# A chunked attention and phase-MLP kernel: the phase weight loaded by SyncE in fp32 and cast on chip, and another order of all work

## The chip, the cores and the metric

The kernel runs on one core of one Trainium2 chip. The time is device microseconds of one execution; the figure given for a kernel is the median of its runs. Lower is better.

## The reference

Two parts follow each other. The first is attention in chunks of 64 rows, the second mixes tokens and channels with cosines and sines.

```python
# q, k, v: (8, 8, 576, 64)
scores = (1 / sqrt(64)) * q_c @ k_c.T            # per batch, head and chunk of 64 rows
attn = softmax(scores)
x = (attn @ v_c), heads side by side             # (8, 576, 512)

theta = x @ w_theta                              # (512, 512)
zr, zi = x * cos(theta), x * sin(theta)
y = w_tok_r @ zr + w_tok_i @ zi                  # (576, 576) over the tokens
u = x + y
out = u + max(u @ w_ch, 0)                       # float32
```

## The kernel before, in words

The eight batches are taken as four pairs, numbered 0 to 3. The 1152 rows of a pair are nine tiles of 128 rows: groups A and B (two tiles each) of the first batch, C and D of the second, and M, one tile made of the last 64 rows of both. Nearly everything is computed in fp16 with sums in fp32.

The program is written out by hand. `ORDER` is a list of steps, and the last loop of the kernel runs through it under a manual schedule; each step records its instructions at once, so the order of the list is the order in each engine's queue. Each engine takes its own queue in order and waits at an instruction until what it needs is there. A step has the form `kind.pair-and-group.bank`; the PSUM banks (eight, of 512 fp32 columns) are chosen in the list too. A digit 0 or 1 at the end of a kind means one half of a step. The kinds that matter here:

- `qF`, `kF`, `q`, `k` and `v` (lines L181, L194, L222 and L232) load by POOL's queue, which casts fp32 to fp16 on the way. A whole group's q or k is 512 KB in HBM and 256 KB on chip. `lw` loads the token weights (L243), `lc` the channel weight (L254), `lt` the phase weight theta (`load_theta`, L251). From pair 1 on, `gate` (L170) makes POOL copy one number of the latest reciprocal of `norm` before a load is issued, which ties the loads to the progress of the attention.
- `F` (L301), `FL` (L316), `L` (L339) and `N` (L335) turn q and k on TensorE by transposes against an identity. `F` does a group with 64 transposes of 64x64, `FL` with 32 of 128x64. For group M, `L` takes 16 and `N` 8.
- `tq` and `tqA` copy the turned q from PSUM (VectorE L368, ScalarE L370), `tkV` and `tkA` the turned k (L368, L372).
- `S` is the scores (L405), `e` the exponential (L422), `V` the product with v (L440), with a column of ones for the sum, and `n` the reciprocal and the scaling (VectorE, L452 and L454).
- `X` (L478) and `Q` (L487) turn x: 8 transposes of 128x128, or 32 of 64x64. `U` and `R` do the same with u. `xA`, `xV`, `uA` and `uV` copy the result on ScalarE or VectorE (L501).
- `H` is x times theta (L518), `g` cosine and sine (ScalarE, L532 and L536), `z` the two products (VectorE, L548 and L549).
- `TW` turns the token weights (L269). For pair 0, `YA` to `YD` and `YM` mix the tokens directly (L604); for pairs 1 to 3 it is done by seven products `Ka` to `Kg` and `Km` over differences of blocks (L693), with the differences made by `ja` to `jd` and the results taken by `ra` to `rh` (VectorE, L712). `Y` is the mixing of group M (L590), `y` the sum with x.
- `W` is u times the channel weight (L518), `w` adds the positive part (VectorE, L733), `s` and `sA` store by SyncE's and ScalarE's queue (L748 and L744).
- `D` issues dummy products of zeros on TensorE (L280); `pe` and `pg` call the exponential's or the sine's table on ScalarE.

The pool `nat` has ten buffers, which groups' q and k, the token weights, the differences of `j` and the last output tiles take in turn.

Of the kernel before, what the change touches and what calls it, by code (L numbers as in the profile page):

```python
# [9 lines left out]
FP32 = mybir.dt.float32  # L10
# [18 lines left out]
n0.1C kF.2A lc.00 tkA.1B YA.0A.6 V1.1A.0 n1.1A V0.1A.4 YB.0A.6 v.1M V1.1C.0 n0.1A S.1B.2 L.1M.4
qF.2C e.1B X.1A.5 qF.2D xA.1A n1.1C X.1C.0 kF.2C YM.0A.6 U.0D.1 H.1A.2 xV.1C pg.00 g.1A tq.1M  # L30
uV.0D H.1C.0 tkV.1M kF.2D F.1D.5.4 tkA.1D y.0A jw.01 v.2A R.0C.6 g.1C tq.1D uV.0C YA.0B.2 S.1D.4
V0.1B.6 YM.0B.2 n0.1B z.1C YB.0B.2 e.1D y.0B FL.2A.0 qF.2B tqA.2A V1.1D.6 q.2M V0.1D.4 n0.1D
W.0D.2 S.1M.4 k.2M n1.1D w.0D X.1D.6 kF.2B TW.04.7 tkA.2A e.1M v.2D twV.04 V1.1M.0 V0.1M.1
S.2A.2 xA.1D e.2A V1.1B.4 n1.1B n0.1M z.1A H.1D.6 n1.1M X.1B.5 pg.00 g.1D xV.1B W.0C.2 w.0C
ja.1C R.0A.0 X.1M.4 uA.0A sA.0C z.1D qF.3A jc.1D U.0B.5 H.1B.6 uA.0B v.2C g.1B xA.1M W.0A.0
Ka.1A.2 w.0A F.2C.4.5 F.2D.0.1 ra.1A tq.2D tkA.2C tkA.2D sA.0D jb.1D qF.3D Y.0M.7 V0.2A.0 n0.2A
z.1B tqA.2C H.1M.6 y.0M N.2M.4 tkA.2M g.1M Kf.1C.2 S.2D.0 tqA.2M F.2B.7.6 V1.2A.4 rc.1C n1.2A
z.1M v.3D e.2D tqA.2B kF.3D Kg.1D.2 rg.1B X.2A.0 xV.2A Ke.1C.4 re.1D tkA.2B v.2M Km.1D.2 qF.3B
U.0M.1 rf.1D H.2A.6 pg.00 g.2A uV.0M Kc.1D.4 jd.1B S.2C.0 pe.00 e.2C q.3M v.2B s.0A rd.1C
V0.2D.6 n0.2D Y.1M.2 S.2B.6 kF.3A y.1M V0.2C.0 n0.2C e.2B k.3M Kb.1B.4 z.2A V1.2C.6 qF.3C kF.3C  # L40
S.2M.0 e.2M n1.2C W.0B.2 rb.1A V1.2D.0 n1.2D Q.2C.6 W.0M.4 U.1C.5 w.0B s.0B v.3A w.0M U.1A.0
uV.1C X.2D.1 xA.2C H.2C.2 xV.2D V1.2M.4 V0.2B.6 uA.1A V0.2M.5 pg.00 g.2C n1.2M n0.2B H.2D.0
W.1A.6 g.2D n0.2M Q.2M.4 xA.2M F.3A.2.3 F.3D.0.1 z.2C w.1A V1.2B.4 n1.2B tkA.3D W.1C.6 tqA.3A
ja.2C z.2D X.2B.1 w.1C H.2M.2 xA.2B Kd.1B.4 tkA.3A tqA.3D g.2M H.2B.6 rh.1B v.3C s.0M S.3A.0
jb.2D kF.3B R.1D.2 Ka.2A.4 g.2B v.3B Ke.2C.6 z.2M uA.1D ra.2A Kf.2C.4 F.3C.2.3 e.3A V0.3A.0
jc.2D tkA.3C re.2D n0.3A tqA.3C rc.2C Kc.2D.6 rd.2C V1.3A.0 n1.3A S.3D.2 e.3D Kg.2D.4 z.2B rg.2B
S.3C.6 s.1A e.3C Q.3A.0 W.1D.2 U.1B.6 v.3M Km.2D.4 xA.3A H.3A.0 w.1D rf.2D V0.3C.2 n0.3C R.1M.4
uV.1M uA.1B W.1B.6 sA.1C jd.2B F.3B.2.3 N.3M.4 pg.00 g.3A z.3A w.1B Kb.2B.0 tqA.3B tkA.3B
V1.3C.2 tqA.3M rb.2A S.3B.6 pe.00 e.3B Y.2M.5 n1.3C tkV.3M Q.3C.0 xA.3C V0.3D.6 y.2M n0.3D
S.3M.2 W.1M.4 e.3M w.1M U.2C.5 uA.2C V1.3D.0 V1.3M.2 n1.3D s.1B V0.3M.3 n0.3M n1.3M H.3C.6 pg.00  # L50
g.3C V0.3B.0 sA.1M Q.3D.4 xV.3D Kd.2B.2 n0.3B rh.2B V1.3B.0 n1.3B R.2D.6 uA.2D W.2C.4 w.2C
# [10 lines left out]
def kernel(  # L62
# [22 lines left out]
    GT = 2 * P  # L85
# [20 lines left out]
    nat = ctx.enter_context(tc.tile_pool(name="nat", bufs=10))  # L106
# [60 lines left out]
    def gate(p):  # L167

        if p and marks:
            nc.gpsimd.tensor_copy(out=seen, in_=marks.pop())  # L170
            marks.clear()

    def load_qk(p, g, which, plain, f=None):
        j0, bb, s0 = GROUPS[g]
        gate(p)
        if (p, g) not in nats:
            nats[p, g] = nat.tile([P, 2, 2 * DM], FP16, name="qk16", tag="nat")
        if plain is None:
# [12 lines left out]
        if bb is None:
            t = t[:, 0:DM].rearrange("p (h d) -> p h d", h=H)
            for b in range(2):
                nc.gpsimd.dma_start(  # L194
                    t[half[b]], ap[2 * p + b, :, s0 : s0 + CH, :].rearrange("h s d -> s h d")
                )
            return
        if plain:
            t = t.rearrange("p (j h d) -> p j h d", j=2, h=H)
            for j in range(2):  # L200
                t0 = s0 + j * P
                nc.gpsimd.dma_start(
                    t[:, j, hs],
                    ap[2 * p + bb, :, t0 : t0 + P, :].rearrange("h s d -> s h d"),
                )
            return

        nc.gpsimd.dma_start(
            t.rearrange("p (h x) -> p h x", h=H)[:, hs],
            ap[2 * p + bb, :, s0 : s0 + GT, :].rearrange(  # L210
                "h (p s) d -> p h (s d)", s=2
            ),
        )
# [525 lines left out]
    def store(p, g, f, queue):  # L739
# [71 lines left out]
    with tc.manual_schedule():  # L811
        for step in ORDER:
# [5 lines left out]
            p, g = int(at[0]), int(at[1]) if at[1].isdigit() else at[1]  # L818
# [36 lines left out]
```

## Time and profile before

| | |
|---|---|
| median of 3 runs | 203.94 us (202.31 to 204.08) |
| the profiled execution | 205.1 us, of which the span of the instructions is 203.3 us |
| TensorE busy | 186.4 us (92%), 3567 matmuls |
| VectorE / ScalarE / POOL busy | 150.3 / 124.4 / 83.3 us |
| loads by POOL's queue | 65408 packets, 16.54 MB, 85.9% of 16 engines' span |
| stores by SyncE's and ScalarE's queues | 4.72 MB each, 6.4% and 6.5% |
| granted TensorE clock | 0.999 |

The span starts with the first instruction of the program and ends with the last; the execution has 1.8 us around it. In the views, L numbers are lines of the kernel before, and a DMA's landing is the time at which its completion was signalled. The busy time of TensorE counts dummies too.

### The profile page before, as it was taken

How to read it: one execution, taken by the hardware profiler on the slowest of the kernel's cores; microseconds unless marked ns; L12 is line 12 of the kernel's file. 1: busy time of each engine (PE TensorE's matmuls, PEld its weight loads, DVE VectorE, ACT ScalarE, POOL GpSimd, SP SyncE). 2: the span in 40 equal slices, each digit the busy share in tenths (PEclk: the TensorE clock that was granted, in tenths of full speed). 3: DMA queues.
4: the chain of work that ended last, by engine and by line, in shares of the span. 5: the costliest groups of instructions: out<-in, count | busy, mean ns of one | idle time of the engine just before them, and what ended most of it. 6: DMA issues, size and time to landing. Idle time of an engine off the chain costs nothing.

```text
span 203.3 us, 7900 instructions
## 1 busy us (share of the span) xinstructions
PE 186.4 (92%) x3567; PEld 99.6 (49%) x3567; DVE 150.3 (74%) x238; ACT 124.4 (61%) x150; POOL 83.3 (41%) x134
## 2 busy tenths in 40 slices
PE   7677587999989979999999999999999999999990
PEld 2345445555455545555455564455555544445530
DVE  0042738975766869989988888979988899889480
ACT  2354577995168869679673978956889366001510
POOL 7875957749959675105956137002000000000000
PEclk9999999999999999999999999999999999999999
DMA  5999999999999999962999929505121002004875
GB/s 62 177 191 146 157 141 196 195 175 121 167 178 182 175 128 104 221 223 23 136 141 129 228 108 124 34 3 77 59 106 41 19 3 103 0 0 157 298 286 194
DMA packets 70433, 26.48 MB, mean 130 GB/s; under 512 B 47232, under 2 KB 65792, under 8 KB 70400
## 3 DMA queue, kind: packets, MB, share of 16 engines
q0 software_dynamic: 65408, 16.54, 85.9%
q10 hardware_dynamic: 2496, 4.72, 6.5%
q1 hardware_dynamic: 2496, 4.72, 6.4%
q8 instruction: 28, 0.46, 0.9%
q14 instruction: 5, 0.04, 0.1%
HBM read 33.06 MB, written 9.44 MB: 209 GB/s over the span
## 4 chain that ended last, share of the span: by engine, by line
PE 84%; DMA 4%; POOL 3%; issue 3%; ACT 2%; DVE 1%; ACTq 0%; POOLq 0%
PE ps L518 32%; PE ps L693 21%; PE ps L604 8%; DMA qk<-in_k_dram 4%; PE ps L590 4%; PE ps L478 4%; PE ps L440 3%; PE ps L301 3%; PE ps L487 3%; PE ps L405 3%; POOL qk L181 2%; PE ps L269 2%; POOL v L232 1%; ACT kT L372 1%; PE ps L316 1%
## 5 line engine op out<-in xcount | busy, mean ns | idle before, releaser
L232 POOL DMA_DIRECT2D v<-in_v_dram x48 | 36.3, 778 | 3.6 <-DMA qk<-in_k_dram 2.0
L518 PE MATMUL ps<-wch,uT 128*128 128x512 f16 x144 | 34.1, 380 | 1.2 <-issue 1.2
L518 PE MATMUL ps<-wtheta,xT 128*128 128x512 f16 x144 | 34.5, 380 | 0.0
L712 DVE TENSOR_TENSOR x<-ps,x 128x1024 f16<-128x1024 f32 x24 | 29.1, 1221 | 4.6 <-PE ps L693 4.1
L501 ACT COPY uT<-ps 128x1024 f16<-128x1024 f16 (+1 forms) x14 | 13.6, 982 | 25.8 <-PE ps L487 18.7
L733 DVE SCALAR_TENSOR_TENSOR o<-ps,x 128x1024 f32<-128x1024 f32 (+1 forms) x20 | 22.2, 1115 | 6.7 <-PE ps L518 6.4
L454 DVE TENSOR_TENSOR x<-ps,recip 128x512 f16<-128x512 f32 (+1 forms) x40 | 25.5, 638 | 1.4
L532 ACT ACTIVATE cos<-ps,pihalf 128x1024 f16<-128x1024 f32 (+1 forms) x22 | 21.1, 959 | 6.8 <-PE ps L518 5.8
L422 ACT ACTIVATE eT<-ps 128x1024 f16<-128x1024 f32 (+1 forms) x18 | 16.5, 926 | 11.5 <-PE ps L405 11.2
L372 ACT COPY kT<-ps 128x1024 f16<-128x1024 f16 (+1 forms) x18 | 16.3, 922 | 9.6 <-PE ps L301 5.5
L518 PEld LDWEIGHTS <-uT 128*128 128x128 f16 x144 | 13.1, 98 | 16.2 <-issue 1.7
L518 PEld LDWEIGHTS <-xT 128*128 128x128 f16 x144 | 12.9, 98 | 13.6
L536 ACT ACTIVATE sin<-ps 128x1024 f16<-128x1024 f32 (+1 forms) x22 | 19.0, 865 | 0.0
L693 PE MATMUL ps<-z,wT 128*128 128x512 f16 x72 | 18.8, 379 | 0.0
L170 POOL COPY seen<-recip 1x1 f32<-1x1 f32 x16 | 3.2, 199 | 37.4 <-DVE recip L452 37.4
L452 DVE RECIPROCAL recip<-ps 128x8 f32<-128x8 f32 (+1 forms) x40 | 7.9, 198 | 12.7 <-PE ps L440 11.9
L604 PE MATMUL ps<-z,wT 128*128 128x512 f16 x72 | 16.9, 380 | 0.1
L368 DVE COPY qT<-ps 128x1024 f16<-128x1024 f16 (+2 forms) x11 | 6.4, 581 | 14.3 <-PE ps L316 9.3
L693 PE MATMUL ps<-zsum,wsum 128*128 128x512 f16 x72 | 16.7, 379 | 0.2 <-DVE x L712 0.2
L693 PEld LDWEIGHTS <-wsum 128*128 128x128 f16 x96 | 9.1, 98 | 10.5 <-issue 0.2
L693 PEld LDWEIGHTS <-wT 128*128 128x128 f16 x96 | 9.1, 98 | 10.3
L370 ACT COPY qT<-ps 128x1024 f16<-128x1024 f16 (+2 forms) x12 | 9.9, 823 | 6.5 <-PE ps L316 5.8
(68 smaller groups left out, 294.3 us busy)
## 6 DMA issues: line engine op xcount, KB each, us to landing
qk<-in_q_dram POOLq DMA_DIRECT2D x16, 256.0 KB, 6.0
qk<-in_k_dram POOLq DMA_DIRECT2D x16, 256.0 KB, 6.7
out_dram<-o ACTq DMA_DIRECT2D x8, 512.0 KB, 4.9
out_dram<-o SPq DMA_DIRECT2D x8, 512.0 KB, 3.7
v<-in_v_dram POOLq DMA_DIRECT2D x40, 64.0 KB, 5.3
v<-in_v_dram POOLq DMA_DIRECT2D x16, 128.0 KB, 5.7
wnat<-in_moe_w_tok_r_dram POOLq DMA_DIRECT2D x2, 288.0 KB, 5.8
wnat<-in_moe_w_tok_i_dram POOLq DMA_DIRECT2D x2, 288.0 KB, 6.3
```

What stands on the lines that cost most here:

```text
L232: nc.gpsimd.dma_start(v16[rows, slot + tile, :, 0:D], v[2 * p + bb, :, t0 : t0 + m, :].rearrange("h s d -> s h d"),)
L372: nc.scalar.copy(out=t.rearrange("p x s c -> p x (s c)").rearrange("p x (c s) -> p x c s", s=n), in_=ps.rearrange("p x s c -> p x c s"),)
L422: nc.scalar.activation(out=eT.rearrange("p h r e c -> p (h r e) c"), in_=ps, func=AF.Exp, scale=scale)
L454: nc.vector.tensor_tensor(out=tokens(p, g, "x")[:, :, f * NE * D : (f + 1) * NE * D].rearrange("p c (h d) -> p c h d", h=NE), in0=psv[:, 0 ...
L501: (nc.vector.tensor_copy if how == "V" else nc.scalar.copy)(out=to.rearrange("p b (r c) -> p b r c", c=CH), in_=psv)
L518: nc.tensor.matmul(ps[:, a * DM : a * DM + cols.stop - cols.start], xT[:, b0 + a, db, :], weight[:, db, cols], start=(db == 0), stop=(db = ...
L532: nc.scalar.activation(out=cos[:, 0:n].rearrange("p a e -> p (a e)"), in_=pin, func=AF.Sin, bias=pihalf, scale=1.0,)
L536: nc.scalar.activation(out=sin[:, 0:n].rearrange("p a e -> p (a e)"), in_=pin, func=AF.Sin)
L604: nc.tensor.matmul(ps[:, a * DM : a * DM + DM], wT[:, kt, t0 : t0 + P], zs[bb], start=(done + k == 0), stop=(done + k == NK - 1),)
L693: nc.tensor.matmul(ps[:, a * DM : a * DM + DM], wt, zt, start=fresh and i == 0, stop=i == len(terms) - 1, skip_group_check=to in ("x", "z"),)
L712: nc.vector.tensor_tensor(out=u, in0=st[p]["ps_k", frm], in1=u, op=ALU.add)
L733: nc.vector.scalar_tensor_tensor(out=o, in0=ps[:, 0 : n * m].rearrange("p (j d) -> p j d", j=n), scalar=0.0, in1=u, op0=ALU.max, op1=ALU.add,)
```

## The change

The phase weight is no longer loaded by POOL with a cast on the way. `load_theta` takes two buffers of `nat`, and SyncE issues two loads of 512 KB in fp32 into them, without a wait ahead of them. A new step `ct` casts a half to fp16: `ctA1` the second half on ScalarE, `ctV0` the first half on VectorE.

`ORDER` is another one throughout. The groups of pair 0 come as C, D, A, B, M (before: A, D, C and B, M). Eight whole groups are turned by `F` and six by `FL` (before 13 and 1); `X` is used 12 times and `Q` twice (before 8 and 6), `U` and `R` 8 times each (before 6 and 10), with group M's counted apart; all of group M's turns of q and k are `N`. Five q copies go from VectorE to ScalarE, four u copies from ScalarE to VectorE. There are 43 dummies (before 33), 30 of them ahead of the first turn, and one table call fewer. TensorE has 3233 pairs of weight load and matmul instead of 3567.

```diff
 ORDER = """
-qF.0A kF.0A id.00 init.00 D.12.0 qF.0D D.5.0 FL1.0A.0 kF.0D FL0.0A.2 tqA1.0A tq0.0A tkA1.0A
-S1.0A.0 tkA0.0A F.0D.7.6 tq.0D tkA.0D D.5.2 S.0D.2 e1.0A S0.0A.4 e0.0A v.0A qF.0C D.2.0 V0.0A.0
-qF.0B V1.0A.4 n0.0A kF.0B D.6.0 FL0.0B.0 e.0D FL1.0B.2 kF.0C F.0C.6.7 tkA0.0B tqA0.0B n1.0A
-X1.0A.4 tkA.0C tq1.0B v.0D X0.0A.5 D.3.0 V0.0D.0 tq.0C q.0M k.0M n0.0D lt.00 xV0.0A tkA1.0B
-S1.0B.2 V1.0D.6 n1.0D e1.0B S.0C.0 L0.0M.2 L1.0M.3 e.0C tkV0.0M tkV1.0M X.0D.5 xV.0D tq1.0M
-tqA0.0M S0.0B.0 e0.0B S0.0M.6 S1.0M.0 e1.0M H.0D.2 xV1.0A e0.0M v.0C V0.0C.0 V1.0C.4 pg.00 g.0D
-n0.0C n1.0C H1.0A.7 H0.0A.6 v.0B V1.0B.0 n1.0B v.0M lw.02 Q.0C.4 xA.0C g1.0A V0.0M.2 n0.0M g0.0A
-V0.0B.0 V1.0M.3 H.0C.4 lw.00 qF.1C kF.1C n0.0B X0.0B.0 n1.0M qF.1A kF.1A X1.0B.1 z.0D xV1.0B
-Q.0M.2 xA.0M qF.1B kF.1B v.1C TW.02.6 twV.02 H.0M.3 g.0C TW.03.1 twA.03 q.1M k.1M xV0.0B z1.0A
...
-Q.3B.0 xV.3B R.2B.6 z.3C uA.2B H.3D.2 g.3D R.2A.0 ja.3C uA.2A Q.3M.6 xA.3M z.3D jb.3D H.3B.4
-Ka.3A.2 ra.3A H.3M.0 g.3M z.3M Ke.3C.6 Kf.3C.2 sA.2C re.3D rc.3C W.2A.0 g.3B z.3B w.2A Kc.3D.6
-rd.3C W.2D.4 w.2D jc.3D Kb.3B.0 W.2B.4 jd.3B Kg.3D.2 rb.3A Kd.3B.0 rg.3B Km.3D.2 w.2B R.3A.6
-rh.3B s.2B Y.3M.4 rf.3D s.2A y.3M uA.3A sA.2D R.3C.0 R.3D.2 R.3B.6 W.3A.4 uA.3C w.3A W.3C.0 w.3C
-uA.3B sA.1D U.3M.4 uA.3D W.3D.2 s.3A w.3D W.3B.0 sA.3C R.2M.2 sA.3D uV.3M w.3B s.3B W.3M.4 w.3M
-s.3M uA.2M W.2M.7 w.2M sA.2M
+qF.0C lt.00 id.00 qF.0D kF.0C init.00 D.12.0 D.18.0 FL.0C.0 kF.0D ctA1.00 tqA.0C FL.0D.2 tkA.0D
+tq.0D tkA.0C D.8.6 S.0D.6 e.0D S.0C.0 qF.0A kF.0A FL1.0A.2 tkA1.0A v.0D D.2.4 V0.0D.4 n0.0D
+V1.0D.6 n1.0D D.3.4 X.0D.4 xV.0D e.0C tqA1.0A FL0.0A.0 tq0.0A tkA0.0A v.0C V0.0C.6 n0.0C ctV0.00
+S0.0A.0 S1.0A.2 e1.0A e0.0A qF.0B kF.0B FL1.0B.4 q.0M tq1.0B FL0.0B.6 tq0.0B k.0M V1.0C.2 n1.0C
+N0.0M.0 N1.0M.1 tkV1.0M tkA1.0B S1.0B.4 tqA0.0M X.0C.2 tkA0.0B tkV0.0M S0.0M.6 e1.0B e0.0M
+tq1.0M v.0A xV.0C V1.0A.0 S1.0M.4 e1.0M v.0M S0.0B.2 e0.0B v.0B V0.0A.6 n0.0A H.0D.4 V0.0M.2
+pg.00 g.0D V1.0M.3 n1.0A X1.0A.0 H.0C.6 g.0C lw.02 lw.00 qF.1C kF.1C V1.0B.4 qF.1B n0.0M V0.0B.1
+xV1.0A X0.0A.0 n1.0M H1.0A.3 qF.1A kF.1A xV0.0A kF.1B H0.0A.0 v.1B X.0M.6 n0.0B g1.0A TW.02.1
+n1.0B X0.0B.7 TW.03.4 xA.0M v.1A X1.0B.3 H.0M.6 z.0D twV.03 TW.00.4 z1.0A xA0.0B H0.0B.7 g0.0A
+v.1C twV.02 xA1.0B z.0C qF.1D kF.1D F.1C.0.1 YD.0D.2 twA.00 g.0M lc.00 tkA.1C YC.0D.2 TW.01.4
+q.1M k.1M H1.0B.1 g0.0B tq.1C v.1D F.1A.0.6 z.0M z0.0A lw.04 g1.0B twV.01 YM.0A.4 z1.0B z0.0B
+tkA.1A v.1M YA.0A.4 v.2B YM.0D.2 YB.0A.4 qF.2C tqA.1A qF.2D kF.2D y.0D S.1A.6 qF.2B y.0A FL.1B.0
+pe.00 e.1A S.1C.2 V0.1A.4 n0.1A YD.0C.6 e.1C YM.0C.6 V0.1C.2 FL.1D.4 n0.1C jw.00 tkA.1B qF.3A
+kF.3A tqA.1B S.1B.0 e.1B V1.1A.2 tqA.1D tkA.1D YC.0C.6 U.0A.0 kF.2C n1.1A uV.0A YA.0B.2 V1.1C.0
...
+W.0D.0 N.2M.2 ra.1A tkA.2M Kf.1C.4 z.1M Ke.1C.6 tqA.2M w.0D rc.1C tqA.2A v.2A S.2A.0 e.2A re.1D
+jc.1D FL.2D.2 tqA.2D tkA.2D jd.1B Kc.1D.6 rd.1C V0.2A.0 n0.2A S.2D.2 e.2D Kg.1D.4 Kb.1B.6 sA.0B
+rg.1B F.2B.0.1 Km.1D.4 v.2D R.1C.2 rb.1A sA.0C tkA.2B V1.2A.6 n1.2A uA.1C tqA.2B rf.1D Y.1M.1
+qF.3D V0.2C.2 n0.2C X.2A.0 y.1M S.2B.6 e.2B V1.2D.4 n1.2D W.1C.2 S.2M.4 w.1C qF.3C kF.3C V1.2C.6
+n1.2C xA.2A H.2A.0 e.2M pg.00 g.2A R.0M.2 V0.2D.4 V0.2M.6 U.1A.7 uV.0M W.0M.3 s.0D n0.2D X.2D.2
+V1.2M.4 xA.2D uV.1A w.0M V1.2B.0 n1.2B U.1D.5 n1.2M X.2C.7 n0.2M s.1C uA.1D xA.2C H.2D.2 Q.2M.0
+g.2D F.3A.4.5 V0.2B.6 k.3M xV.2M H.2C.0 g.2C Kd.1B.2 n0.2B X.2B.6 z.2A z.2D xA.2B Ka.2A.0 tqA.3A
+kF.3D z.2C W.1A.6 tkA.3A H.2M.4 s.0M rh.1B H.2B.2 g.2M ja.2C g.2B ra.2A v.3D jb.2D Kf.2C.0 w.1A
...
+rh.2B xV.3C V1.3B.0 Y.2M.4 n1.3B z.3A z.3D V0.3B.0 n0.3B y.2M R.2C.2 uA.2C H.3C.6 W.2C.2 g.3C
+R.2A.0 uA.2A Q.3B.4 Ka.3A.6 w.2C R.2B.0 xA.3B uA.2B z.3C ja.3C jb.3D s.1M Q.3M.4 xA.3M H.3B.2
+W.2B.0 jc.3D g.3B ra.3A H.3M.5 z.3B Ke.3C.2 g.3M re.3D Kf.3C.6 z.3M rc.3C sA.1B jd.3B s.1D w.2B
+sA.2B W.2A.4 Kc.3D.2 w.2A rd.3C Kg.3D.6 rg.3B Kb.3B.0 Kd.3B.2 rb.3A Km.3D.6 R.3A.0 Y.3M.4 s.2D
+uA.3A rh.3B rf.3D R.3D.0 y.3M uV.3D R.3B.6 R.3C.2 uV.3B W.3A.4 w.3A s.2C uV.3C W.3B.0 U.2M.7
+sA.2A w.3B W.3D.4 w.3D uV.2M s.3A W.3C.0 w.3C s.3B U.3M.2 uA.3M s.3D sA.3C W.2M.7 w.2M sA.2M
+W.3M.2 w.3M s.3M
 """.split()
...
     v16 = glob.tile([P, 2 * NT, H, VP], FP16, name="v16")
+    wraw = []
     wnat = {}
...
     def load_theta():
-        nc.gpsimd.dma_start(wtheta16, moe_w_theta.rearrange("(a p) e -> p a e", p=P))
+        for a in range(2):
+            t = nat.tile([P, 2, DM], FP32, name="wraw", tag="nat")
+            wraw.append(t)
+            nc.sync.dma_start(
+                t, moe_w_theta[a * GT : a * GT + GT, :].rearrange("(a p) e -> p a e", p=P)
+            )
+
+    def cast_theta(a, copy):
+        copy(out=wtheta16[:, 2 * a : 2 * a + 2], in_=wraw[a])
...
+        "ctA": lambda p, g, f: cast_theta(f, nc.scalar.copy),
+        "ctV": lambda p, g, f: cast_theta(f, nc.vector.tensor_copy),
```

More of the change, by code (lines that the diff above doesn't have):

```diff
@@ L23 @@
-n0.0C n1.0C H1.0A.7 H0.0A.6 v.0B V1.0B.0 n1.0B v.0M lw.02 Q.0C.4 xA.0C g1.0A V0.0M.2 n0.0M g0.0A
-V0.0B.0 V1.0M.3 H.0C.4 lw.00 qF.1C kF.1C n0.0B X0.0B.0 n1.0M qF.1A kF.1A X1.0B.1 z.0D xV1.0B
-Q.0M.2 xA.0M qF.1B kF.1B v.1C TW.02.6 twV.02 H.0M.3 g.0C TW.03.1 twA.03 q.1M k.1M xV0.0B z1.0A
-z.0C H1.0B.0 v.1A g.0M z0.0A qF.2A v.1D TW.01.6 twV.01 H0.0B.1 g0.0B z.0M TW.00.4 F.1C.3.2 tq.1C
-twA.00 jw.00 YD.0D.6 g1.0B z1.0B YC.0D.6 F.1A.0.1 tkA.1C S.1C.2 pe.00 e.1C YM.0C.4 tq.1A YM.0D.6
-y.0D YC.0C.4 tkA.1A z0.0B F.1B.0.1 qF.1D kF.1D V0.1C.2 v.1B S.1A.6 lw.04 tq.1B YD.0C.4 e.1A y.0C
@@ L29 @@
[L29 to L51, printed above, removed]
-Q.3B.0 xV.3B R.2B.6 z.3C uA.2B H.3D.2 g.3D R.2A.0 ja.3C uA.2A Q.3M.6 xA.3M z.3D jb.3D H.3B.4
@@ new lines @@
+kF.3A tqA.1B S.1B.0 e.1B V1.1A.2 tqA.1D tkA.1D YC.0C.6 U.0A.0 kF.2C n1.1A uV.0A YA.0B.2 V1.1C.0
+qF.2A y.0C S.1D.4 e.1D kF.2A X.1A.7 YB.0B.2 q.2M V0.1D.4 n1.1C V1.1B.0 xA.1A n0.1D n1.1B YM.0B.2
+y.0B kF.2B H.1A.6 TW.04.0 twV.04 k.2M N.1M.5 tq.1M X.1C.4 U.0B.0 tkV.1M pg.00 g.1A uV.0B W.0A.2
+z.1A V0.1B.0 n0.1B S.1M.6 pe.00 e.1M w.0A Y.0M.5 V1.1D.6 n1.1D v.2M s.0A xA.1C X.1B.0 H.1C.2
+pg.00 g.1C xV.1B v.3C X.1D.0 jw.01 y.0M xV.1D z.1C v.3B W.0B.6 U.0D.5 U.0C.0 H.1D.2 uA.0D
+F.2C.1.4 uV.0C w.0B g.1D tqA.2C V0.1M.0 n0.1M V1.1M.5 n1.1M W.0C.6 X.1M.5 H.1B.2 xA.1M v.2C
@@ new lines @@
+tkA.2C ja.1C z.1D w.0C H.1M.0 g.1B jb.1D Ka.1A.4 z.1B S.2C.6 q.3M g.1M F.2A.3.2 tkA.2A e.2C
+W.0D.0 N.2M.2 ra.1A tkA.2M Kf.1C.4 z.1M Ke.1C.6 tqA.2M w.0D rc.1C tqA.2A v.2A S.2A.0 e.2A re.1D
[3 more added lines that the diff above has]
+n1.2C xA.2A H.2A.0 e.2M pg.00 g.2A R.0M.2 V0.2D.4 V0.2M.6 U.1A.7 uV.0M W.0M.3 s.0D n0.2D X.2D.2
@@ new lines @@
+V1.2M.4 xA.2D uV.1A w.0M V1.2B.0 n1.2B U.1D.5 n1.2M X.2C.7 n0.2M s.1C uA.1D xA.2C H.2D.2 Q.2M.0
+g.2D F.3A.4.5 V0.2B.6 k.3M xV.2M H.2C.0 g.2C Kd.1B.2 n0.2B X.2B.6 z.2A z.2D xA.2B Ka.2A.0 tqA.3A
+kF.3D z.2C W.1A.6 tkA.3A H.2M.4 s.0M rh.1B H.2B.2 g.2M ja.2C g.2B ra.2A v.3D jb.2D Kf.2C.0 w.1A
+qF.3B v.3A S.3A.6 jc.2D rc.2C z.2M e.3A F.3C.4.5 tkA.3C Ke.2C.2 Kg.2D.0 kF.3B re.2D tqA.3C
+FL.3D.6 z.2B tqA.3D rg.2B Kc.2D.2 rd.2C U.1M.5 Km.2D.0 rf.2D tkA.3D S.3D.6 sA.1A U.1B.4 v.3M
+e.3D W.1D.2 uA.1B w.1D uA.1M N.3M.0 tqA.3M V0.3A.6 V1.3A.4 U.2D.1 uA.2D Kb.2B.2 n1.3A n0.3A
@@ new lines @@
+X.3A.1 tkA.3M rb.2A W.1M.0 w.1M S.3M.6 xA.3A V0.3D.4 e.3M n0.3D F.3B.2.3 tqA.3B W.2D.0 jd.2B
+V1.3D.4 w.2D n1.3D S.3C.6 tkA.3B e.3C H.3A.2 V0.3C.0 V0.3M.7 V1.3M.4 n1.3M n0.3C pg.00 g.3A
+W.1B.5 X.3D.4 n0.3M w.1B xV.3D Kd.2B.0 V1.3C.2 S.3B.4 H.3D.6 n1.3C Q.3C.2 pe.00 e.3B pg.00 g.3D
+rh.2B xV.3C V1.3B.0 Y.2M.4 n1.3B z.3A z.3D V0.3B.0 n0.3B y.2M R.2C.2 uA.2C H.3C.6 W.2C.2 g.3C
+R.2A.0 uA.2A Q.3B.4 Ka.3A.6 w.2C R.2B.0 xA.3B uA.2B z.3C ja.3C jb.3D s.1M Q.3M.4 xA.3M H.3B.2
+W.2B.0 jc.3D g.3B ra.3A H.3M.5 z.3B Ke.3C.2 g.3M re.3D Kf.3C.6 z.3M rc.3C sA.1B jd.3B s.1D w.2B
```

## The prediction

> **What bounds the kernel now.** I read the page's engine line first, then busy time in six stretches, then the chain of waits, then the DMA landings and the instruction queue's packets.
>
> ```profile
> PE 186.4 (92%) x3567; PEld 99.6 (49%) x3567; DVE 150.3 (74%) x238; ACT 124.4 (61%) x150; POOL 83.3 (41%) x134
> ```
>
> ```profile
> core 0: us, PE busy (x) PEld busy (x) DVE busy (x) ACT busy (x) POOL busy (x), PEclk, DMA share, GB/s
> 0.00:25.30 25.30, 17.73 (x465) 10.40 (x465) 8.16 (x21) 11.11 (x17) 19.91 (x33) 1.00 1.45 146
> 25.30:41.00 15.70, 14.08 (x281) 8.18 (x276) 11.24 (x28) 12.82 (x19) 10.59 (x18) 1.00 1.49 179
> 41.00:75.00 34.00, 31.91 (x758) 17.82 (x744) 23.81 (x41) 22.86 (x27) 25.96 (x43) 1.00 1.71 162
> 75.00:125.00 50.00, 49.75 (x922) 27.02 (x922) 44.25 (x69) 38.53 (x45) 24.68 (x40) 1.00 1.15 142
> 125.00:198.00 73.00, 72.90 (x1176) 36.16 (x1173) 62.17 (x82) 39.09 (x45) 2.21 (x4) 1.00 0.33 86
> ```
>
> TensorE is the bound from 25.3 us to 198 us: 49.75 of 50.00 and 72.90 of 73.00 us busy. No other engine is near its limit over a whole stretch. What can be won lies ahead of 25.3 us, in the idle 3.7 us of the next two stretches, or in TensorE's own work. The last matmul ends at 197.9; 5.4 us of adding and storing follow.
>
> ```profile
> 8.18 8.83 DMA qk<-in_k_dram
> 17.00 0.39 issue
> 17.40 0.65 PE ps L316 x16
> ...
> 27.38 0.55 issue
> ...
> 33.97 0.43 issue
> ...
> 58.03 0.81 issue
> ...
> 68.38 1.01 PE ps L316 x32
> ...
> 71.39 1.21 issue
> ...
> 92.00 1.24 DVE x L712
> ...
> 95.16 0.45 PE ps L478 x8
> ...
> 118.28 1.08 PE ps L301 x128
> ...
> 160.54 0.64 PE ps L487 x64
> ```
>
> Columns: start, us, what. Two things stop TensorE: the load stream (group B's k at 17.0) and pauses called "issue" with no releaser. The pauses sit at TensorE's records 705, 961, 1217, 2241 and 2753 in order: each 193 more than a multiple of 256. The instruction queue brings 28 packets of 16 KB, 256 instructions each, so a pause is a block of instructions that came late. Ahead of 75 us, while the load queue is full, a block's packet begins about 4 us after the block before it was entered, and the block is usable about 2.5 us after that; five of ten blocks made TensorE wait, 3.9 us together.
>
> **The change, part by part.**
>
> *Theta (L250 to 251).* Before, POOL issues it at 18.57, and it lands at 24.40, 2.85 us behind the transfer ahead of it; everything after it in the queue (v.0C, v.0B, v.0M, lw) is that much later. After, SyncE issues two fp32 halves of 512 KB at once. The nearest row is a 512 KB store by SyncE at 147.98: first packet 0.89 us after issue, 256 packets of 2 KB at 87 ns, so 1.4 us of all 16 engines. Two halves are 2.8 us of engine time from about 1.8 us on. The load queue's first packet starts at 2.75, and it moves 32 and 177 packets in the slices 2 to 3 and 3 to 4 us against 395 in the next one. So about 1.55 us of the 2.8 fall into free time, and 1.25 us delay the loads. Bounds: 0.5 (all but the overlap is free) to 2.85 (nothing is). I take 1.2, as the idle slices are counted. The stream past pair 0 is then 2.85 - 1.2 = 1.65 us earlier.
>
> The Trainium skill speaks against the move: "DMA: Bandwidth & Descriptors", section "Issuing engines are not separate DMA queues", says that all issuers share the same 16 engines and that spreading saves only issue time. By that alone the delay is the full 2.85 us and the start gains nothing. No run here shows it either way; the idle slices above are what it leaves out.
>
> *Casts.* Half 1 is a ScalarE copy (1.01 us by the 128x1024 copies), first in ScalarE's queue and ahead of tqA.0C. Theta is through by about 6 us, tqA.0C can start at 10.9, so nothing waits. Half 0 is a VectorE copy after n0.0C, about 20.8. No row has its shape: 0.69 (fp16 copy) to 1.22 us (fp32 input), I take 1.0. Behind it stands tq1.0B, for S1.0B; both hide under the wait for v.0A at 24.9. Without that cover it costs its 1.0 us.
>
> *The start in the new order.* 30 dummies (12 at 0.37, 18 at 0.24 us) end at 10.0. q and k of C and D land by 10.01 + 1.2 = 11.2. H.0D now stands behind V1.0A and V0.0A. Ahead of v.0A stand just the 2816 KB that end with k.0M before, at 21.55; with 2.1 us for v itself and 1.2 delay it lands at 24.9, and H.0D starts at 25.4 (25.3 before), with V.0C and X.0C already done. From there the old order lost 0.55 and 0.43 (issue) and 0.65 us (V0.0B for an x of VectorE); the new one has its data in time up to F.1C. k.1C lands at 38.89 - 1.65 = 37.2; YD.0D can start at 37.9, with TW.01 (0.72) and H1.0B (0.87) left over: as good as 39.5, against 41.14. I book -1.4, keeping 0.2 for small waits. By the bounds of the delay: -2.1 to +0.25.
>
> *TensorE's work after 41 us.* A whole "four long" turning (FL) takes 1.01 for 32 transposes, the old F 1.08 to 1.20 for two of 64, so 0.41 more each. After the start there are FL.1B, 1D, 2D, 3D against FL.2A: +1.24. Five Q or R (0.32 each) become X or U (0.45): +0.65. One L (0.57) becomes N (0.45): -0.12. Sum +1.8 (1.5 to 2.1). The 10 added dummies lie in the wait for loads.
>
> *Instruction blocks.* 3567 matmul and weight pairs become 3233. What decides is where the blocks begin. With TensorE's work from the rows above, the new order has 5.6, 6.3, 8.3, 4.0, 8.0, 6.3 and 10.1 us of work between its block borders from V1.0B to U.0C, against some 6.3 us for a block while the loads run. One stands out: the border in YD.0C, 4.0 us after the one in YM.0D. It waits 1.0 to 3.1 us, by blocks that came in 5.0 to 7.1; I take 2.0, and 0.2 for the one at 6.3. Before, the pauses past 41 us were 0.81 + 1.21 = 2.0. Net +0.2; bounds -2.0 (the load queue is thinner, no waits) to +2.5.
>
> The Trainium skill has this fetch in "Runtime: NRT & Kernel Launch", section "Instruction fetch mechanics": blocks of 256 instructions, the crossing mostly hidden. The size agrees; hidden it is not, by the pause of 1.21 us. Were it hidden, this term would be -2.0.
>
> *Other engines.* Five q copies go from VectorE (0.69) to ScalarE (1.02), four u copies back; one sine table load goes. Neither engine becomes a bound: per us of TensorE's work, VectorE has less to do up to any point of the new order than of the old. One new close gate: v.2D waits on POOL for n0.2A's reciprocal, which stands behind rd.1C (1.22) on VectorE. From the end of Kc.1D: 1.5 us to that, 0.5 for POOL, 5.1 from first issue to last landing (94.03 to 99.12 before): 7.1, where V1.2D is due after 8.7. I book 0.4 (0 to 2). Behind V1.2D all of TensorE's queue stands. Tail: the last step is W, w and two small stores as before; 0.
>
> Sum: -1.4 + 1.8 + 0.2 + 0.4 = **+1.0**. The profiled execution has a span of 203.3 and 205.1 us in all, 1.2 above the median of 203.94. Span 204.3, and median 204.9.
>
> **The rivals.**
> - *Theta nearly free and blocks in time.* For it: the idle slices, and 334 fewer pairs. Against: the 4.0 us interval. -2.1 + 1.8 - 2.0 + 0 = -2.3: 201.6.
> - *Theta's megabyte delays the loads by all it takes.* Both queues are shares of the same 16 engines (section 3 of the profile's page), so each packet of theta is one that the loads have to wait for. (The rule that the Trainium skill gives in "DMA: Bandwidth & Descriptors", section "Issuing engines are not separate DMA queues", leads here.) For it: the DMA row is at 9 from 5 us on. Against: the first 4 us are idle. +0.25 + 1.8 + 0.2 + 0.4 = +2.7: 206.6. It decides once v.0A lands after 25.5.
> - *The gate of v.2D.* If VectorE comes to n0.2A with three operations of 1.22 still ahead instead of one, V1.2D waits 2.4 - 1.6 margin, and the later groups gated behind v.2D the same: with the 2 us of the upper bound, +1.0 - 0.4 + 2.0 = +2.6: 206.5. For it: VectorE is at 44.25 of 50 us there. Against: it has more slack in the new order.
>
> **How the numbers follow.** Forecast 0.50, own range 203.0 to 206.5; free theta 0.20; full delay 0.15; gate 0.15. A measurement here can tell about 1%, 2.0 us. Faster: 0.14 of the first rival and 0.03 of the forecast, 0.17. Slower: 0.21 of the two slow rivals and 0.10 of the forecast, 0.31. Within 1%: 0.52. The range for 8 in 10 takes in all three rivals' times and the ends of the unknown costs: 201.4 to 207.8.
>
> **What would show it.** Right: theta landed by 7 us, k of C or D by 11.5, H.0D at 25 to 26, YD.0D at 37.5 to 38.5; one pause of 1 to 3 us in YD.0C; TensorE without gaps after 75 us; four L316 groups of 1.0 us. Wrong: v.0A after 26, a pause at V1.2D, gaps of TensorE past 100 us, or no pause at all.

## The result, and the profile after

| | before | changed |
|---|---|---|
| median of 20 runs each | 203.94 us | 205.49 us |
| lowest and highest run | 201.76 and 208.15 us | 204.39 and 207.04 us |
| ratio, 95% interval | | 1.0106 (1.0080 to 1.0132) |
| profiled execution, and its span | 205.1, 203.3 us | 205.49, 203.7 us |

The changed kernel is slower, by 1.6 to 2.7 us by the ratio. The ratio compares runs within 1.5% of a kernel's lowest, which leaves out six of the 20 of before and none of the changed kernel's; by plain medians the difference is 1.55 us, 0.8%. The profiled execution of before, at 205.1 us, was 1.2 us above its median and that of the changed kernel is at its median, so the two spans, 0.4 us apart, show less than the change costs.

Line numbers are 9 higher than before (those of the loads of q, k and v 1 higher; in e2 and e11 all are 1 higher). The engine line of the page:

```profile
PE 192.6 (95%) x3233; PEld 105.2 (52%) x3233; DVE 148.9 (73%) x236; ACT 124.7 (61%) x151; POOL 81.6 (40%) x130
```

TensorE is busier by 6.2 us with 334 fewer pairs. Part of that is dummies, and part is turns that ran at a granted clock of one half, from 21.8 to 25.3 us. The stretches say where:

```profile
core 0: us, PE busy (x) PEld busy (x) DVE busy (x) ACT busy (x) POOL busy (x), PEclk, DMA share, GB/s
0.00:25.30 25.30, 20.85 (x364) 12.41 (x365) 7.31 (x19) 11.34 (x16) 19.06 (x32) 0.93 1.60 173
25.30:41.00 15.70, 15.32 (x279) 9.03 (x276) 12.56 (x30) 14.55 (x23) 11.60 (x19) 1.00 1.37 176
41.00:75.00 34.00, 34.00 (x593) 19.26 (x592) 24.12 (x44) 23.29 (x29) 24.33 (x38) 1.00 1.64 156
75.00:125.00 50.00, 49.16 (x906) 27.39 (x905) 42.28 (x65) 36.70 (x41) 25.66 (x42) 1.00 1.19 143
125.00:198.00 73.00, 73.00 (x1101) 37.11 (x1098) 61.82 (x82) 38.86 (x45) 0.99 (x2) 1.00 0.33 86
```

From 41 to 75 us TensorE has no gap at all (34.00 of 34.00, before 31.91): the pauses are gone. From 75 to 125 us a new gap of 0.84 us has come. And TensorE ends no earlier. The chain of waits (start, us, what):

```profile
3.92 7.49 DMA qk<-in_k_dram
11.40 0.14 issue
11.54 1.08 PE ps L325 x32
...
49.73 1.01 PE ps L325 x32
...
53.77 1.01 PE ps L325 x32
...
89.01 1.48 POOL v L233 x2
90.49 6.25 DMA v<-in_v_dram
96.74 0.04 issue
...
133.85 1.01 PE ps L325 x32
...
198.34 0.69 DVE o L742
```

Three things are to be seen: the turn of group D waits for its k until 11.40; the `FL` turns of 1.0 us each, of which the old order had one; and in the middle a load, v of group A of pair 2, issued by POOL at 89 and landed at 96.74, in a part where before no load was in the chain.

**A ledger of the two profiled executions.** The mixing step YD.0D starts at 41.14 before and 39.08 after, but after it 1.59 us of TensorE's work (TW.01, H1.0B) is still to do that the old order had done: the start gains 2.06 - 1.59 = 0.47. From YD.0D to the start of the last `W` step it takes 155.73 before and 158.12 after. With the 1.59 put on before's side that is 157.32, of which 2.02 are the pauses at 58.03 and 71.39: 155.3 of work. After, 0.9 is the wait for v of 2A: 157.2. So the work grew by 1.9, the new wait adds 0.9, the pauses take away 2.0, and the last matmul ends 0.34 later (198.24 against 197.90). These are two single executions; the experiments show that both the pauses and the wait come and go from one execution to the next.

### The profile page after: what moved, and what is told of

Read it like the earlier page. It is cut to its first block, busy times and chain, and to the rows that moved or that the text cites. A ratio compares the mean times of both kernels' runs of the same rounds, so it can differ in the third digit from the quotient of the medians.

```text
span 203.7 us, 7222 instructions
## 1 busy us (share of the span) xinstructions
PE 192.6 (95%) x3233; PEld 105.2 (52%) x3233; DVE 148.9 (73%) x236; ACT 124.7 (61%) x151; POOL 81.6 (40%) x130
## 4 chain that ended last, share of the span: by engine, by line
PE 82%; DMA 7%; POOL 4%; DVE 2%; issue 1%; ACT 1%; DVEq 0%; POOLq 0%; ACTq 0%
PE ps L527 30%; PE ps L702 17%; PE ps L613 8%; PE ps L487 6%; PE ps L599 4%; DMA qk<-in_k_dram 4%; PE ps L449 3%; PE ps L325 3%; DMA v<-in_v_dram 3%; PE ps L414 3%; POOL v L233 2%; PE ps L310 2%; PE ps L496 2%; PE ps L289 2%; PE ps L278 1%
## 5 line engine op out<-in xcount | busy, mean ns | idle before, releaser
L510 ACT COPY uT<-ps 128x1024 f16<-128x1024 f16 (+1 forms) x11 | 10.2, 936 | 24.5 <-PE ps L496 14.0
L379 ACT COPY qT<-ps 128x1024 f16<-128x1024 f16 (+2 forms) x16 | 14.3, 902 | 6.8 <-PE ps L325 5.7
L487 PE MATMUL ps<-id,x 128*128 128x128 f16 x196 | 15.6, 220 | 0.5 <-issue 0.5
L487 PEld LDWEIGHTS <-x 128*128 128x128 f16 x196 | 12.2, 98 | 4.4 <-issue 0.7
```

Source lines behind the costliest of these rows:

```text
L487: nc.tensor.transpose(psv[:, b].rearrange("p r c -> p (r c)"), x[:, a0 + j, a * P : a * P + P], id16,)
```

## The experiments

The theory after this first reading: the start gained little because the loads' first landings are late anyway; the work's +1.9 counts in full; 0.9 is the place of v.2A in the load queue; and the pauses of before were those of one execution. Its main rivals: theta's bytes take away the start's gain; the work is hidden or pays by fewer instruction blocks; the old order loses 2 us to pauses in every run. Medians below are of all runs of a kernel, beside that of before in the same batch; ratios are taken as above.

**Theta alone, in the old order** (e1), and **the order alone, theta by POOL** (e2).

```diff
 e1, on before (with the new load_theta and cast_theta)
-qF.0A kF.0A id.00 ... n0.0D lt.00
+qF.0A lt.00 kF.0A id.00 ... FL0.0A.2 ctA1.00 tqA1.0A ... n1.0A ctV0.00 X1.0A.4
 e2, on the changed kernel (with the old load_theta)
-qF.0C lt.00 id.00 ... ctA1.00 ... ctV0.00 ... tq0.0B k.0M
+qF.0C id.00 ... tq0.0B k.0M lt.00
```

Expected of e1: 

> The old order with theta loaded by SyncE at once and cast (second half on ScalarE ahead of the first q copy, first half on VectorE after n1.0A). Theory A (theta falls partly into idle time of the DMA engines; the later loads gain): theta lands by 5.5 us, the first loads land 1.4 us later than before (k.0D at 11.4), v.0C to the token weights 0.5 to 1.5 us earlier; H.0D no longer waits for theta. Time 0.5 to 1.5 us below before. Rival B (the delay of the first loads is all of theta's engine time, so nothing is won): within 0.5 us of before, YD.0D at 41 us or later. Rival C (the fp32 load and the casts cost more than they save): 0.5 us or more above before.

Expected of e2: 

> The new order with theta by POOL as before (behind k.0M, where the old order has it) and no casts. Theory A: theta's 2.85 us come back into the load queue ahead of v.0A, 1.4 us of delay at the start go: H.0D starts about 1.5 us later than in the changed kernel, and the time is 1.0 to 1.5 us above the changed kernel, 3 to 4 above before. Rival B (theta's place is worth nothing): within 0.5 us of the changed kernel. Rival C: below the changed kernel.

Measured: e1 204.20 us beside 204.63, ratio 1.0064 (1.0028 to 1.0100); e2 208.42 beside 204.63, ratio 1.0264 (1.0218 to 1.0309). The timeline of TensorE in e1 and in e2 (start, us, line, operation, and in brackets the idle time before it and its releaser):

```profile
8.51 1.08 PE L325 MATMUL ps<-id,qk 128*64 128x128 f16 x32 [2.04 <-DMA qk<-in_k_dram]
```

```profile
28.43 1.14 PE L441 MATMUL ps<-v,eT 64*64 64x65 f16 x16 [2.78 <-DMA v<-in_v_dram]
30.16 3.15 PE L519 MATMUL ps<-wtheta,xT 128*128 128x512 f16 x7
```

In the old order the moved theta stands in front of the first k: the first turn starts at 8.51 instead of 6.82, k.0D lands at 11.12 instead of 10.01 (11.01 in a second profile of before, e12), and the first H starts at 27.47 instead of 25.32. But YD.0D starts at 41.96, within the 41.14 to 42.24 of before, e4, e10 and e12, so by then nothing of the loss is left. By plain medians the kernel is level with before; no gain is shown, and a loss by the ratio alone. In the new order the old place of theta costs far more: it lands at 26.80, v.0A behind it makes TensorE wait 2.78 us, and YD.0D starts at 43.73 instead of 39.08. The time is 2.9 us above the changed kernel, twice the upper end of what was expected. So the two halves of the change belong together: the order alone costs 2.6%, and the move of theta takes 1.6 points of that back.

**No theta at all** (e11) and **the identity later** (e8). Both ask what makes k.0D late.

```diff
 e11, on the changed kernel: theta is neither loaded nor cast, its tile is filled with 0.01 by VectorE
-qF.0C lt.00 id.00 ... ctA1.00 ... ctV0.00
+qF.0C id.00 ... init.00 lt.00
 e8, on the changed kernel
-qF.0C lt.00 id.00 qF.0D kF.0C
+qF.0C lt.00 qF.0D id.00 kF.0C
```

Expected of e11: 

> The changed kernel without theta's load and casts: VectorE fills the fp16 weight with a constant instead, so the phases are not the reference's; all else is as it was. Theory A (in the new order theta's two loads are covered, since the load queue stands idle behind its first load anyway): the first four loads land within 0.3 us of the changed kernel's, and the time is within 0.4 us of it. Rival B (theta's 1.2 to 1.4 us of delay are real here too): k of D lands by 10.3 us, H.0D starts 1 us earlier or more, and the time is 0.7 us or more below.

Expected of e8: 

> The changed kernel with POOL's making of the identity behind the second load and not behind the first. In the runs so far k of D lands at 10.0 us without theta and the identity behind two loads, at 11.1 with theta, and at 11.5 without theta and 11.4 with it when the identity stands behind one load. Theory A (the two delays cover each other: either the identity or theta takes the same idle time of the load queue): the four first loads land 0.2 to 0.5 us earlier than in the changed kernel, and the time is within 0.5 us of it. Rival B (the delays add up): 1.0 to 1.5 us earlier, and the time 0.5 to 1.5 us below.

Measured: the first four loads land at 5.48, 8.12, 9.63 and 11.03 in e11, where k.0D is the fourth, and at 7.08, 8.49, 9.98 and 11.40 in the changed kernel. Theta's megabyte holds up the first load by 1.6 us and the fourth by 0.4. k.0M lands at 23.43 without theta and 23.45 with it. In e11 the second load comes 2.64 us after the first, the others 1.4 to 1.5 us apart, and between the issue of the first and second POOL writes the identity (before: behind the second load). Since k.0D also varies between executions of one start, all profiles are put together:

| k.0D lands at, us | identity behind two loads | identity behind one |
|---|---|---|
| no theta ahead of it | 9.76, 10.01, 10.40, 11.01 (e10, before, e4, e12) | 11.03, 11.53 (e11, e2) |
| theta by SyncE | 11.12, 11.52 (e1, e8) | 11.40 to 12.01, mean 11.62 (changed kernel, e3, e5, e6, e7, e9) |

By the means, theta alone makes k.0D 1.0 us later, the identity's place alone 1.0, and both together 1.3: the two delays cover each other. The groups that are loaded first differ between the orders as well, and the spread within one field reaches 1.25 us, so the sizes are rough. In time, e8 is 205.49 beside 204.65 (1.0101, 1.0060 to 1.0142), the changed kernel's; e11 204.96 beside 204.45 (1.0059, 1.0018 to 1.0101), 0.5 us below the changed kernel by medians, with intervals that overlap: whether theta still costs something in another way is open.

**A warm clock** (e5). In slice 5 of the page the granted clock fell for 3.41 us:

```profile
PEclk9999699999999999999999999999999999999999
```

```diff
 e5, on the changed kernel: more dummies
-D.3.4 X.0D.4 ... V0.0C.6 n0.0C
+D.8.3 X.0D.4 ... V0.0C.6 D.5.3 n0.0C
```

> The changed kernel with dummies in the two idle stretches of TensorE at 16.6 and 20.4 us (eight in place of three after V1.0D, five new ones after V0.0C, in a free bank). Theory A (the half clock granted from 21.8 to 25.3 us follows from the idle time ahead of it, and it delays H.0D): the granted clock stays at 1.0 past 5 us, H.0D starts 0.5 to 1.5 us earlier, and the time is 0.5 to 1.2 us below the changed kernel. Rival B (H.0D waits for v.0A and its chain, not for TensorE's speed): H.0D at the same time within 0.3 us and the time within 0.4 us of the changed kernel.

Measured: 205.66 beside 204.65, 1.0108 (1.0041 to 1.0175). The clock is 1.00 from 5.4 to 200 us, and the first H starts at 27.58, not earlier than 27.05. TensorE waits 1.05 us until 24.99 instead, which the trace puts down to a load of v. In time nothing is gained. That the dummies kept the clock up is not shown by this one execution: e6, e7 and e9 have the changed kernel's start without them, and no slow stretch either. They start H.0D at 25.6 to 26.6, so whether the stretch costs something at the changed kernel's place stays open. In e3, e8 and e11 the stretch of 3.41 us comes later, from 26.2 to 26.6 on. There it does cost, since it covers products: the first H takes 2.9 to 3.3 us instead of 1.9, and YD.0D starts at 40.4.

**The turns: `F` for `FL` in the new order** (e3, e6), **`FL` for `F` in the old** (e4).

```diff
 e3, on the changed kernel          e6: the last two lines alone
-FL.1B.0
+F.1B.0.1
-FL.1D.4
+F.1D.4.5
-FL.2D.2
+F.2D.2.3
-FL.3D.6
+F.3D.6.7
 e4, on before
-F.1C.3.2 ... F.1A.0.1 ... F.1B.0.1 ... F.1D.5.4
+FL.1C.2 ... FL.1A.0 ... FL.1B.0 ... FL.1D.4
```

Expected of e3: 

> The changed kernel with F in place of FL for groups 1B, 1D, 2D and 3D, in the same banks. Theory A (TensorE is the bound, a whole FL takes 1.01 us and an F 0.5 to 0.6): 1.6 to 2.0 us below the changed kernel, at the level of before or under it. Rival B (the 128 added pairs of weight load and matmul make blocks of instructions late): pauses called issue come back in the trace, each 0.4 to 1.2 us, and the gain is 0 to 1 us or turns into a loss.

Expected of e4: 

> The kernel before with FL in place of F for 1C, 1A, 1B and 1D. Theory A (TensorE's work counts in full): 1.6 to 2.0 us above before. Rival B (128 pairs fewer let the blocks of instructions arrive in time): the pauses at 58.03 and 71.39 of the trace before, 2.0 us together, are gone or moved, and the time is within 0.7 us of before or below it.

Expected of e6: 

> The changed kernel with F in place of FL for groups 2D and 3D alone, which come after 90 us, where the load queue is no longer full; 1B and 1D stay FL. Theory A (FL pays only while blocks of instructions are slow; after that it is 0.4 us of TensorE each): no new pause called issue, 0.6 to 0.9 us below the changed kernel. Rival B (the shift of the block borders or the added instructions cost there too): the same as the changed kernel or above it.

Measured: e3 208.64 beside 204.63, 1.0256 (1.0200 to 1.0313); e4 205.07, 1.0102 (1.0050 to 1.0153); e6 205.35 beside 204.65, 1.0089 (1.0052 to 1.0127). Taking the longer turns out should have won 1.6 us and lost 3 by medians. The timeline of TensorE in e3:

```profile
54.91 0.72 PE L310 MATMUL ps<-id,qk 64*64 64x64 f16 x64
55.44 0.28 PE L414 MATMUL ps<-qT,kT 64*64 64x64 f16 x11
58.12 0.37 PE L414 MATMUL ps<-qT,kT 64*64 64x64 f16 x21 [2.40 <-issue]
```

A pause of 2.40 us with no releaser, at TensorE's record 1985, 193 more than a multiple of 256 as in every other pause of any run here. TensorE stopped 3.9 us after it had passed the border before, and the packet of the block began 3.7 us after that border: the more but shorter turns bring the borders closer together than this block could follow. In e6, which has the shorter turns only behind 90 us, there is no new pause, and it wins 0.14 us by medians and 0.35 by the ratio, where 0.6 to 0.9 was expected. Half of that is missing for a reason that the timeline of e6 shows:

```profile
92.08 0.73 PE L310 MATMUL ps<-id,qk 64*64 64x64 f16 x64
93.26 1.02 PE L702 MATMUL ps<-z,wsum 128*128 128x512 f16 x4 [0.45 <-DVE x L721]
```

Behind the turn of 2D comes Kc.1D, and with the shorter turn it waits 0.45 us for VectorE, which still takes an earlier product. So 64 small transposes are 0.4 us cheaper than 32 large ones, but at 2D TensorE only waits for it, and among the loads of pair 1 the 32 more pairs each cost more than the time.

By the Trainium skill ("Runtime: NRT & Kernel Launch", section "Instruction fetch mechanics") blocks hold 256 instructions and their crossing is mostly hidden. The spacing of 256 agrees with every pause here; this crossing was not hidden, it cost 2.40 us.

In the old order the four long turns remove the pauses past 41 us (windows of e4):

```profile
41.00:75.00 34.00, 34.00 (x668) 19.67 (x663) 24.42 (x44) 23.78 (x28) 25.41 (x42) 1.00 1.75 167
```

and yet it is no faster: 1.0% slower by the ratio, 0.4 us by medians. So the pauses that it saves are worth less than the work that it adds. That asks how large they are without it:

**The kernel before, once more** (e12).

> The kernel before, unchanged, for a second profile of it. The first profiled execution took 205.1 us in all where the median is 203.94, and lost 2.0 us past 41 us in two pauses called issue. Theory A (the pauses belong to the execution, not to the kernel: the same blocks of instructions come late in one and in time in another): less than 1 us of such pauses past 41 us, and a span of 201.5 to 202.8 us. Rival B (they belong to the order): the same two pauses in U.0D and W.0D, 2.0 us within 0.5, and a span of 203 us or more.

Measured: 202.89 us for the profiled run, with a span of 201.0, and 205.95 for the only other one. The profiled run:

```profile
41.00:75.00 34.00, 33.77 (x805) 19.17 (x806) 25.33 (x46) 24.68 (x28) 26.81 (x44) 1.00 1.74 164
75.00:125.00 50.00, 49.75 (x959) 26.99 (x960) 44.35 (x66) 37.62 (x46) 25.34 (x40) 1.00 1.22 149
```

The same program loses 0.23 us from 41 to 75 us here, where the profiled execution of before lost 2.09. So the pauses are not in every execution of this program: two profiles, 2.0 us in one and none in the other. The block that stopped TensorE for 1.21 us in the first (record 2753) had its packet begin 4.3 us after the border before was passed; here it began 1.8 us after, and 5.5 us from border to border were enough. What the longer executions of before lose, no trace shows. Its YD.0D started 0.7 later (41.85), its span is 2.3 us shorter, and 1.9 of the 3.0 us that it takes less from there to the end are these 34 us. From YD.0D to the start of the last `W` step it takes 153.24; e4, with the four longer turns, takes 154.55, so their work counts in nearly full (1.3 of the 1.6 us).

**v.2A earlier in the queue** (e7).

```diff
 e7, on the changed kernel
-g.1C xV.1B v.3C X.1D.0 ... z.1C v.3B W.0B.6 ... tqA.2A v.2A S.2A.0
+g.1C xV.1B v.2A X.1D.0 ... z.1C W.0B.6 ... tqA.2A v.3C v.3B S.2A.0
```

> The changed kernel with v.2A in the place of v.3C in the load queue, and v.3C and v.3B in the place of v.2A; these two are needed 30 us later. Theory A (TensorE's 0.9 us at V0.2A are the wait for v.2A, which two loads that are not yet needed stand ahead of): V0.2A takes 0.25 us, and the time is 0.6 to 0.9 us below the changed kernel. Rival B (the wait moves on to V1.2D or another load): within 0.3 us of the changed kernel.

The timeline of TensorE in the changed kernel, and in e7:

```profile
95.75 0.22 PE L449 MATMUL ps<-v,eT 64*64 64x65 f16 x2
96.37 0.19 PE L449 MATMUL ps<-v,eT 64*64 64x65 f16 x1 [0.41 <-DMA v<-in_v_dram]
96.78 0.29 PE L449 MATMUL ps<-v,eT 64*64 64x65 f16 x13 [0.22 <-DMA v<-in_v_dram]
```

```profile
98.08 0.32 PE L449 MATMUL ps<-v,eT 64*64 64x65 f16 x16
98.23 0.42 PE L414 MATMUL ps<-qT,kT 64*64 64x64 f16 x32
```

The product with v does not wait in e7. But this execution started late (YD.0D at 41.46) and came to V0.2A 2.3 us later, so that alone could have spared it the wait. The stretch from 75 to 125 us in e7, and then in e5, whose load queue has v.2A in the old place:

```profile
75.00:125.00 50.00, 49.79 (x917) 27.89 (x916) 43.15 (x68) 37.43 (x42) 25.90 (x40) 1.00 1.19 142
75.00:125.00 50.00, 49.80 (x911) 27.63 (x910) 43.19 (x67) 37.12 (x41) 26.08 (x41) 1.00 1.21 143
```

Both are 49.8 busy instead of 49.16. Of the seven profiled executions with v.2A in the old place, only the changed kernel's and e6's wait at V0.2A, the two with the earliest YD.0D (39.08 and 38.33); e2, e3, e5, e8 and e11 start YD.0D at 39.50 or later and do not. The wait takes back part of an early start. The time of e7 is 204.63 beside 204.65, 1.0061 (1.0018 to 1.0103): by medians 0.86 us below the changed kernel and below e8, which was run beside it, with intervals of the ratio that overlap. A gain is likely; that it is this wait is not shown. By plain medians e7 is level with before, by the ratio 0.6% slower. No version of the new order beat the kernel before.

**Both remedies** (e9): the edits of e7 and e6 together.

> The changed kernel with both edits that lowered it: v.2A earlier in the load queue, and F in place of FL for 2D and 3D. Theory A (the edit to 2D and 3D lost most of its 0.8 us to the wait for v.2A, which is gone here): 1.4 to 1.9 us below the changed kernel, within 0.5 us of before. Rival B (the two edits do not add up, another wait takes the gain of F): at the level of v.2A earlier alone, 0.9 us below the changed kernel.

Measured: 205.19 beside 204.45, 1.0062 (1.0026 to 1.0098). The shorter turns add nothing to e7. The trace has the same wait of 0.45 us for VectorE behind the turn of 2D as e6, so just the 0.4 us of 3D could be won, too little for these runs to tell. Nor do v.2A's place and the turns together come below e11, which has neither and no theta (1.0059 in the same batch).

**The small turns of group M** (e10).

```diff
 e10, on before
-L0.0M.2 L1.0M.3 ... L.1M.4
+N0.0M.2 N1.0M.3 ... N.1M.4
```

> The kernel before with N in place of L for group M of pairs 0 and 1, the one kind of turning in the change that needs both fewer instructions and less of TensorE (0.45 against 0.57 us, 8 transposes in place of 16). Theory A (TensorE is the bound): 0.2 to 0.4 us below before, which can hardly be told from none. Rival B (blocks of instructions decide at the start): the borders move by 16 to 32 pairs, a pause goes or comes, and the time moves by 0.8 us or more.

Measured: 204.68 beside 204.45, 1.0057 (1.0004 to 1.0109); by medians the same as before. From 41 to 75 us it has no pause either (34.00 of 34.00). Its profiled execution had the granted clock at half for 6.83 us from 22.95 on, which hides what little the edit does. This run decides nothing on the work; it only adds an execution of an order close to before's without the 2 us of pauses.

## Why the prediction was right or wrong

The forecast was 204.9 us, and 205.49 came. Way and range were right; the cost was two thirds of what was measured by medians (+1.0 against +1.55) and half by the ratio (+2.2). Not all of that is merit: terms that were wrong by as much as this and more cancelled in part. Point by point:

- **Theta itself: right.** It landed at 4.07 and 5.51 (forecast 6), through the queue of SyncE:

```profile
wraw<-in_moe_w_theta_dram SPq DMA_DIRECT2D x2, 512.0 KB, 3.8
```

- **The landing of k: right in number, half right in reason.** Forecast 11.2 by 1.2 us of theta's delay, measured 11.40. Theta alone does cost about 1.0 where the identity stands behind two loads. But the new order has the identity behind one, which alone costs as much and which the forecast left out; with both, theta adds 0.3 to 0.4. That the two cover each other is luck for the number. The rule of the Trainium skill that was set against the move ("DMA: Bandwidth & Descriptors", section "Issuing engines are not separate DMA queues") would make the delay the full transfer; neither order shows that (0.3 to 1.0 of 2.85), and in the new one the move is worth 1.6 points (e2). In the old order, where no gain was shown (e1), the rule is nearer.
- **The start, -1.4: the step that failed most.** H.0D was to start at 25.4 and started at 27.05, although v.0A landed at 25.10 (forecast 24.9). The forecast had X.0C done by then; in the trace it still stood ahead, with scores and both halves of V.0A behind it (X.0C, V1.0A and H.0D):

```profile
25.27 0.62 PE L487 MATMUL ps<-id,x 128*128 128x128 f16 x8
...
25.90 0.30 PE L449 MATMUL ps<-v,eT 64*64 64x65 f16 x16
...
27.05 1.90 PE L527 MATMUL ps<-wtheta,xT 128*128 128x512 f16 x8
```

  From v.0A's landing to H.0D it took 1.95 us there and 0.9 to 2.2 in the other six executions of this order with theta by SyncE; 0.5 was booked. The stream fell short too: k.1C was to land at 37.2 and landed at 38.41 (before 38.89), 0.5 us earlier and not 1.65. k.0M was 1.9 us later than before (23.45 against 21.55) and not 1.2, and the loads behind it lost 0.5 more. Over these seven executions, against four of the old (before, e4, e10, e12), H.0D starts at 26.9 in the mean against 25.6, k.1C lands at 38.8 against 40.1, and YD.0D starts at 40.0 (38.3 to 41.5); with the 1.59 of work left over that is 41.6, against 41.75. The gain is 0.2, and even the profiled execution's own is 0.47.
- **The work, +1.8: right, if a little low.** The ledger gives +1.9. From YD.0D to the last `W` step, the five executions of e2, e5, e7, e8 and e11, which wait nowhere in between, take 157.05 to 157.30; e12 takes 153.24, with the 1.59 on top 154.83. That makes +2.3, and e4 points the same way.
- **The blocks, +0.2: wrong in two parts that cancelled.** The pause of 2 us in YD.0C did not come. The border there came 5.2 us after the one before (46.82 to 52.06), where 4.0 was booked, and the packet of the next block began within 0.1 us of that border, not 4 us after it; why so early, no run shows. So new pauses cost 0. But the 2.0 that the old order was booked to lose is not in its second profile (e12), nor in e4 and e10; e1 has one pause of 0.47. The term was taken against one execution, 1.2 us above its median, which the text had noted without drawing this from it. It explains why the two spans differ by 0.4 and the medians by more.
- **The gate of v.2D, +0.4: no wait there**, as the range's lower end had it. Where a wait came, it was one place earlier, for v.2A: no gate held it, but two loads for pair 3, first needed 50 us later (V0.3C at 150.45), stand ahead of it in POOL's queue. The prediction looked at gates and not at the queue's own order. It cost 0.9 us in the profiled execution and nothing in five of seven.
- **Casts and tail: right.** VectorE's cast of half a theta took 0.70 us (booked 1.0):

```profile
21.47 0.70 DVE L260 CAST wtheta<-wraw 128x1024 f16<-128x1024 f32 x1
```

  It lies inside the wait for loads. From the last matmul 5.4 us followed, as before.

With what was measured in place of what was booked, between executions without pauses and without the wait: start -0.2 instead of -1.4, work +2.3 instead of +1.8, blocks and gate 0 instead of +0.6. That is +2.1, close to the ratio's +2.2; the medians' +1.55 takes in all runs of before. The sum is made of single executions and shows the sizes, not a second measurement. The forecast's start was 1.2 us too good, and the 0.6 booked for waits that did not come made up half of it.

Of the rivals, the first had its blocks right, and theta's delay behind the identity is nearly nothing; its time was wrong by 4 us, since neither was worth what it was booked at. The second, a full delay by theta, is out by e11, and by e1 too. The third had a wait for a load of pair 2 at the right place; it was another load, held by the queue's order and not by a gate, and not in every execution.

## What to carry to other kernels

Before booking the removal of a pause as a gain, look whether it is there in a second execution: here 2.0 us of "issue" was in one profile and not in the next. The same holds for a wait that one wants to remove: the 0.9 us for v.2A were in two profiles of seven. A load taken out of a full queue is worth what lands earlier at the point where the bound engine next waits, not its transfer time, so follow the stream to that wait. Count also what the bound engine has queued ahead of that point; here it was 0.9 to 2.2 us where 0.5 was booked. And in a hand-made order read the load queue for loads that stand ahead of ones needed sooner.

## What the runs showed of the hardware that was not expected

- The spacing of instruction blocks can outweigh TensorE's work: e3, with shorter turns (0.4 us each) but 32 more pairs at four places, is 3.3 us slower by medians than e6, which has two of them; a single pause in its trace is 2.40 us. All pauses in all runs lie at a record 193 more than a multiple of 256.
- Whether a border costs anything differs between executions of one program: at record 2753 of before 1.21 us in one profile and nothing in e12, where the packet began 2.5 us sooner after the border ahead.
- The granted clock was at half for 3.41 us between 10.9 and 34 us in some executions (changed kernel, e1, e3, e8, e11) or 6.83, twice that (e2, e10), and not at all there in others with the same start (e6, e7, e9). The Trainium skill ("TensorE: Matmul & The Clock Gate", Part 1) has a window of that length, and these stretches agree.
- A megabyte loaded by SyncE ahead of a full software queue delayed that queue's first load by 1.6 us, and its fourth by 0.4 only where POOL's identity stood between the first two (by about 1.0 where it did not).
